# Early loads of chunks 6 and 7, loads behind the transposes in each step, and crossbar transposes for chunks 6 and 7, in a fused retention and feed-forward kernel

One core of one Trainium2 chip. The metric is device time in microseconds (us) of a run; lower is better. A profile gives the span from the first to the last instruction, which is some 1.7 us shorter than the time of the same run (200.26 against 198.6). The granted clock is the share of TensorE's full clock that the trace shows it was given.

## The reference

A recurrent linear attention with a decay per head, then a feed-forward block with a product in place of an activation:

```python
# q, k, v: (4, 8, 768, 64), moe_w1, moe_w2: (512, 1024), w3: (1024, 1024), w_out: (1024, 512)
for t in range(S):
    state = gamma[None, :, None, None] * state + np.einsum('bhd,bhe->bhde', k[:, :, t], v[:, :, t])
    y[:, :, t] = scale * np.einsum('bhd,bhde->bhe', q[:, :, t], state)
x = y.transpose(0, 2, 1, 3).reshape(B * S, H * D)      # 3072 x 512
out = ((x @ w1) * (x @ w2)) @ w3 @ w_out
```

## The kernel before

The kernel folds w3 and w_out into one matrix during the first 31 us, and works through the sequence in 24 chunks of 128 tokens (4 batches of 6). Each chunk needs its queries and keys transposed: chunks 0 to 7 on TensorE, the later ones by transposing DMAs ("by the crossbar"). A step of a chunk computes scores, masks them (VectorE), computes outputs, and pulls matmuls of the feed-forward block in between, so that TensorE has work while other engines answer. All DMAs are issued from one queue (SP; 83408 of the 83430 packets on the page are of its queue q1), in program order: the loads behind the first two stores, at 49.45 and 51.17 us, go out from 51.62 us. Cuts are marked `# ...`.

```python
DT0 = 8                                   # first chunk transposed by the crossbar
for n in range(4, 6):                     # behind the loads of the weights and of chunks 0 to 3
    load_chunk(n)
# ...
def dma_transposes(n):
    if n < DT0 or n >= NSTEP:
        return
    kT = att.tile([128, NP, 128], HP, tag="kT", name="kT", bufs=2)
    nc.sync.dma_start_transpose(kT[:, :, :], k16s[n][:, :])
    # ... even n: the queries of n and n + 1 as well, into qTd

def transposes(n, tag="psT"):
    # ...
    if n >= DT0:
        kT, kp = kTs.pop(n), KP[n % 2]
        nc.scalar.copy(kp[0:64, :, 0, :], kT[0:64, :, :])
        nc.scalar.copy(kp[64:128, :, 1, :], kT[64:128, :, :])
        return
    # ... TensorE transposes into PSUM, then the same two copies

def step(n):
    ready = n * C
    share = fill.available(ready) / (2 - n % 2)
    if n >= DT0 - 2:
        casts(n + 2)                      # GpSimd: q, k, v of chunk n + 2 to 16 bit
    scores(n)
    fill.pull(share * 0.25, ready)
    t_new = kv(n)
    if n < DT0 - 2:
        casts(n + 2)
    dma_transposes(n + 2)
    if n == DT0 - 2:
        load_chunk(n + 4)
    if n % 2:
        q_transposes((n + 1) // 2)        # TensorE, for n + 1 < DT0
    # ...
    outputs(n)
    Tst[0] = t_new
    if n != 4:
        transposes(n + 1)
    fill.pull(share * (0.75 if n == 5 else 0.5), ready)
# ...
load_chunk(6)                             # in program order behind two output stores
load_chunk(7)
# ...
for n in range(4, NSTEP):
    if n != DT0 - 2:
        load_chunk(n + 4)                 # ahead of the step's transposes
    step(n)
```

## Time and profile before

| | before |
|---|---|
| time, first three runs | 198.48, 198.84, 201.69 us (median 198.84) |
| the profiled run | 200.26 us, span 198.6 us, granted clock 0.991 |
| TensorE busy | 187.5 us, 94% |

The slices, windows and timelines that matter are shown in the prediction. In a line of a timeline the columns are start, duration (us), engine, source line, operation, output<-inputs; in brackets is the engine's idle time before it and what ended it.

### The profile page before, as it was taken

The numbers are of one execution on the slowest core, as the hardware profiler recorded it, in microseconds if no ns is written. First come the engines' busy times: TensorE is split into PE (matmuls) and PEld (weight loads), VectorE is DVE, ScalarE is ACT, GpSimd is POOL, SyncE is SP. The second block draws the span as 40 slices with busy tenths as digits, with TensorE's granted clock in tenths as the row PEclk, the third lists the DMA queues.
The fourth block names the chain that finished last, engine by engine and source line by source line (L and its number), as shares of the span: only waits on it lengthen the run. The fifth ranks groups of instructions, "written<-read, shape, count | busy, mean of one in ns | idle before, by whom it ended". The sixth has DMA issues, their size and how long they took to land.

```text
span 198.6 us, 4708 instructions
## 1 busy us (share of the span) xinstructions
PE 187.5 (94%) x1789; PEld 141.9 (71%) x1789; DVE 119.0 (60%) x223; ACT 98.6 (50%) x191; POOL 85.8 (43%) x146
## 2 busy tenths in 40 slices
PE   6899989799999999599999999999999999999993
PEld 2444658486897798388778877787778777887752
DVE  3227596899597666356647665665567665853220
ACT  6478454762445452454455545554546345633322
POOL 7600477827557568244723256646234442200000
PEclk9999999999999999789999999999999999999999
DMA  5999999993699999994998999979999832111014
GB/s 206 377 385 382 311 393 321 373 251 76 178 239 214 195 236 216 210 241 122 199 237 214 190 187 232 201 181 191 204 240 196 175 78 59 56 53 52 35 37 143
DMA packets 83430, 40.15 MB, mean 202 GB/s; under 512 B 59728, under 2 KB 78416, under 8 KB 83408
## 3 DMA queue, kind: packets, MB, share of 16 engines
q1 hardware_dynamic: 83408, 39.86, 86.5%
q8 instruction: 14, 0.23, 0.5%
q14 instruction: 8, 0.07, 0.1%
HBM read 29.36 MB, written 6.29 MB: 180 GB/s over the span
## 4 chain that ended last, share of the span: by engine, by line
PE 66%; DMA 17%; SPq 4%; DVE 3%; POOL 3%; ACT 2%; issue 2%; POOLq 0%; ACTq 0%; DVEq 0%
PE psF L503 32%; PE psO L529 17%; DMA v<-in_v_dram 6%; DMA stg<-in_moe_w_dram 5%; DMA q<-in_q_dram 4%; PE psA L432 4%; SPq L62 4%; DMA kT<-k 3%; PE psY L472 2%; PE psY L473 2%; PE psY L475 2%; PE psK L455 2%; POOL q L327 1%; PE psF L710 1%; PE psW L293 1%
## 5 line engine op out<-in xcount | busy, mean ns | idle before, releaser
L503 PE MATMUL psF<-xt,w 128*128 128x256 f16 (+1 forms) x736 | 86.3, 268 | 0.0
L503 PEld LDWEIGHTS <-w 128*128 128x128 f16 x768 | 68.8, 99 | 7.7
L519 DVE TENSOR_TENSOR ht<-pa,psF 128x256 f16<-128x256 f32 x88 | 36.6, 417 | 27.6 <-PE psF L503 13.8
L513 ACT COPY pa<-psF 128x256 f32<-128x256 f32 x84 | 31.3, 372 | 35.4 <-PE psF L503 35.0
L437 DVE TENSOR_TENSOR am<-psA,keep 128x512 f16<-128x512 f32 x48 | 31.0, 686 | 21.3 <-PE psA L432 21.0
L529 PE MATMUL psO<-w3o,ht 128*128 128x512 f16 x184 | 43.1, 379 | 0.0
L464 POOL TENSOR_TENSOR t<-s,GS 128x512 f16<-128x512 f32 x15 | 19.3, 1285 | 46.6 <-DVE s L463 46.6
L534 ACT ACTIVATE osb<-psO 128x512 f32<-128x512 f32 x23 | 13.8, 598 | 34.4 <-PE psO L529 34.4
L529 PEld LDWEIGHTS <-ht 128*128 128x128 f16 x184 | 17.9, 98 | 17.1 <-DVE ht L759 0.2
L344 POOL TENSOR_TENSOR vp<-v,VS 128x256 f16<-128x256 f32 x40 | 23.8, 616 | 11.7 <-PE psY L475 5.8
L327 POOL CAST q<-q 128x1024 f16<-128x1024 f32 x12 | 13.0, 1087 | 16.2 <-DMA q<-in_q_dram 16.2
L480 DVE TENSOR_TENSOR xt<-psY,YS 128x512 f16<-128x512 f32 x24 | 17.8, 741 | 3.5 <-PE psY L475 3.2
L432 PEld LDWEIGHTS <-kp 128*128 128x128 f16 x192 | 12.7, 99 | 7.5 <-ACT kp L406 2.2
L472 PE MATMUL psY<-am,vp 128*128 128x128 f16 x96 | 16.8, 219 | 0.7 <-ACT kp L230 0.5
L473 PE MATMUL psY<-am,vp 128*128 128x128 f16 x96 | 16.7, 219 | 0.4 <-DVE vp L318 0.4
L340 POOL CAST k<-k 128x512 f16<-128x512 f32 x20 | 12.3, 613 | 7.5 <-PE psK L455 7.0
L463 DVE TENSOR_TENSOR s<-psK,t 128x512 f32<-128x512 f32 x16 | 11.0, 688 | 3.4 <-PE psK L455 3.1
L432 PE MATMUL psA<-qTd,kp 128*128 128x128 f16 x128 | 10.3, 224 | 2.1 <-ACT kp L406 1.7
L406 ACT COPY kp<-kT 64x512 f16<-64x512 f16 x16 | 9.9, 619 | 4.7 <-DMA kT<-k 4.4
L251 DVE COPY w3t<-psW 128x1024 f16<-128x1024 f16 x8 | 5.5, 691 | 10.2 <-PE psW L259 7.9
L473 PEld LDWEIGHTS <-vp 128*128 128x128 f16 x96 | 9.4, 98 | 1.4 <-POOL vp L318 0.7
L475 PE MATMUL psY<-qTd,t 128*128 128x128 f16 x56 | 10.1, 219 | 0.0
(80 smaller groups left out, 198.6 us busy)
## 6 DMA issues: line engine op xcount, KB each, us to landing
stg<-in_moe_w_dram SPq DMA_DIRECT2D x16, 512.0 KB, 7.7
q<-in_q_dram SPq DMA_DIRECT2D x12, 512.0 KB, 4.8
out_dram<-osb SPq DMA_DIRECT2D x23, 256.0 KB, 2.3
k<-in_k_dram SPq DMA_DIRECT2D x20, 256.0 KB, 5.2
v<-in_v_dram SPq DMA_DIRECT2D x20, 256.0 KB, 5.7
stg<-in_moe_w_out_dram SPq DMA_DIRECT2D x4, 512.0 KB, 7.4
stg<-in_k_dram SPq DMA_DIRECT2D x2, 512.0 KB, 10.7
stg<-in_v_dram SPq DMA_DIRECT2D x2, 512.0 KB, 8.2
```

The lines of the kernel that those rows point to most:

```text
L327: nc.gpsimd.tensor_copy(q16[:, :].rearrange("i (t h d) -> i h t d", t=2, d=D), q_in.pop(m)[:, :].rearrange("i (h t d) -> i h t d", t=2, d=D),)
L344: nc.gpsimd.tensor_tensor(vp[:, :, r, r * 64 : r * 64 + 64], v32[:, :].rearrange("j (p s e) -> j p s e", s=2, e=64)[:, :, r, :], VS[:, :]. ...
L432: nc.tensor.matmul(ps[:, i, r, :], lhsT=kp[:, p, r, :], rhs=queries(n, p), start=True, stop=True)
L437: nc.vector.tensor_tensor(am[:, half * 2 : half * 2 + 2, :, :].rearrange("j p s i -> j (p s) i"), ps[:, :, :, :].rearrange("j p s i -> j ( ...
L464: eng.tensor_tensor(t16[:, :, :], s32[:, :, :], GS[:, :, :], MULT)
L472: nc.tensor.matmul(ps[:, p, :], lhsT=vp[:, p, 0, :], rhs=am[:, p, 0, :], start=True, stop=False)
L473: nc.tensor.matmul(ps[:, p, :], lhsT=vp[:, p, 1, :], rhs=am[:, p, 1, :], start=False, stop=(c == 0))
L480: nc.vector.tensor_tensor(XT[n // 2][:, :, n % 2 * C : (n % 2 + 1) * C].rearrange("p a (i t) -> p a t i", t=2), ps[:, :, :].rearrange(orde ...
L503: nc.tensor.matmul(ps[:, i * w : (i + 1) * w], lhsT=W[d][:, (f + i) * 128 : (f + i + 1) * 128], rhs=XT[self.tok0 // TB][:, d, c0 : c0 + w] ...
L513: nc.scalar.copy(self.pa[f][:, :], ps[:, :])
L519: nc.vector.tensor_tensor(self.HT[:, f : f + TB // self.width, :].rearrange("p f n -> p (f n)"), self.pa.pop(f)[:, :], ps[:, :], MULT,)
L529: nc.tensor.matmul(psO[:, :], lhsT=self.HT[:, f, tb * 128 : (tb + 1) * 128], rhs=W3O[f][:, :], start=(f == 0), stop=(f == 7),)
```

## The change

The intent: put the loads of chunks 6 and 7 where the DMA has little to do (a share of 0.15 from 47 to 51.6 us), so that its backlog at chunk 9 goes away; and, as the data is there earlier, let the crossbar take transposes of chunks 6 and 7 from TensorE. Keys of 7 stay on TensorE.

```diff
-    DT0 = 8
+    DT0 = 6
@@
-    for n in range(4, 6):
+    for n in range(4, 8):
         load_chunk(n)
@@
+    def by_dma(n):
+        return n >= DT0 and n != DT0 + 1
@@ dma_transposes, transposes: keys by the crossbar if by_dma(n), not if n >= DT0
@@ step
         dma_transposes(n + 2)
-        if n == DT0 - 2:
-            load_chunk(n + 4)
+        load_chunk(n + 4)
@@
-        if n != 5:
-            fill.pull(share * 0.25, ready)
+        fill.pull(share * 0.25, ready)
@@
-        fill.pull(share * (0.75 if n == 5 else 0.5), ready)
+        fill.pull(share * 0.5, ready)
@@ head: kv(0) moves from ahead of w3_mm(7) into its middle, with scores(1) and outputs(0)
@@
-    load_chunk(6)
-    load_chunk(7)
@@
     for n in range(4, NSTEP):
-        if n != DT0 - 2:
-            load_chunk(n + 4)
         step(n)
```

More of the change, by code (lines that the diff above doesn't have):

```diff
@@ L384, in dma_transposes @@
             return
-        kT = att.tile([128, NP, 128], HP, tag="kT", name="kT", bufs=2)
-        nc.sync.dma_start_transpose(kT[:, :, :], k16s[n][:, :])
-        kTs[n] = kT
+        if by_dma(n):
+            kT = att.tile([128, NP, 128], HP, tag="kT", name="kT", bufs=2)
+            nc.sync.dma_start_transpose(kT[:, :, :], k16s[n][:, :])
+            kTs[n] = kT
         if n % 2 == 0:
@@ L403, in transposes @@
             return
-        if n >= DT0:
+        if by_dma(n):
             kT, kp = kTs.pop(n), KP[n % 2]
@@ L682, with chunk1_scores @@
     scores(0)
-    t_new = kv(0, "psT")
     cast_w(W1, w1_st, 2, False)
-    w3_mm(7, lambda: [scores(1), outputs(0)])
-    Tst[0] = t_new
+    def chunk1_scores():
+        first.append(kv(0, "psT"))
+        scores(1)
+        outputs(0)
+    first = []
+    w3_mm(7, chunk1_scores)
+    Tst[0] = first[0]
     outputs(1, "psT")
```

## The prediction

> **What bounds the kernel now.** I read the page first (busy shares, the slices), then the chain that ended last, then the windows, and only then the timelines of the places where TensorE stops.
>
> ```profile
> PE 187.5 (94%) x1789; PEld 141.9 (71%) x1789; DVE 119.0 (60%) x223; ACT 98.6 (50%) x191; POOL 85.8 (43%) x146
> PE   6899989799999999599999999999999999999993
> PEclk9999999999999999789999999999999999999999
> PE 66%; DMA 17%; SPq 4%; DVE 3%; POOL 3%; ACT 2%; issue 2%; POOLq 0%; ACTq 0%; DVEq 0%
> ```
>
> TensorE is busy 94% of the span, so there is little to win but its idle time and its own work. Of the 11.1 us that it is not busy, the slices show three places: the first 40 us, where weights arrive; one slice at 5 tenths, the 17th (79 to 84 us), which is also where the granted clock dips to 7 and 8 tenths; and the last slice. The windows of four stretches confirm it:
>
> ```profile
> 40.57:79.88 39.31, 39.27 (x466) 32.62 (x465) 29.49 (x55) 16.93 (x35) 24.11 (x33) 1.00 1.03 196
> 79.88:90.57 10.69, 8.54 (x66) 6.32 (x66) 4.65 (x9) 4.83 (x10) 4.13 (x7) 0.84 1.18 221
> 90.57:175.10 84.53, 84.53 (x820) 67.55 (x819) 53.59 (x102) 43.21 (x91) 35.91 (x48) 1.00 0.87 172
> ```
>
> The columns are length, then busy time of TensorE, its weight loads, VectorE, ScalarE and GpSimd, then clock, DMA share and GB/s. From 40.6 to 195 us TensorE never stops except in the middle line. So whatever is saved in that line, and whatever TensorE work goes after 40.6 us, comes off the end one for one. What stops it is in the timelines of TensorE and of ScalarE, and the chain of waits:
>
> ```profile
> 78.16 1.89 PE L529 MATMUL psO<-w3o,ht 128*128 128x512 f16 x8
> 81.80 0.23 PE L432 MATMUL psA<-qTd,kp 128*128 128x128 f16 x1 [1.74 <-ACT kp L406]
> 82.43 0.93 PE L432 MATMUL psA<-qTd,kp 128*128 128x128 f16 x7 [0.41 <-ACT kp L407]
> 83.15 2.77 PE L503 MATMUL psF<-xt,w 128*128 128x256 f16 x12
> 81.12 0.62 ACT L406 COPY kp<-kT 64x512 f16<-64x512 f16 x1 [4.37 <-DMA kT<-k]
> 75.89 5.21 DMA kT<-k
> ```
>
> The scores of chunk 9 wait for the copy of its keys, and the copy for the crossbar transpose that was issued at 75.89 us and took 5.21 us. **The size of the hole:** a step of the steady loop takes 6.56 us from one group of psO matmuls to the next (89.00, 95.56 in the chain); here it took 88.84 - 78.16 = 10.68 us. The loss is 4.12 us: 2.15 us of idle time, the rest the restart at half clock (12 matmuls of 128x256 in 2.56 us of start-to-start time here, 1.31 us in other steps, and scores at the same ratio).
>
> Why was the transpose so late? Its source, the cast of chunk 9's keys, was done at about 68.0 us (the GpSimd timeline has that cast at 67.41, 0.61 long). But the DMA queue's timeline shows an unbroken row of issues from 51.17 to 80.8 us:
>
> ```profile
> 54.24 1.44 SPq L62 DMA_DIRECT2D k<-in_k_dram  x1
> ...
> 56.91 2.46 SPq L62 DMA_DIRECT2D q<-in_q_dram  x1
> ...
> 65.92 1.91 SPq L386 DMA_TRANSPOSE kT<-k  x1
> 67.88 1.29 SPq L390 DMA_TRANSPOSE qTd<-q  x1
> ...
> 74.71 1.09 SPq L536 DMA_DIRECT2D out_dram<-osb  x1
> 75.89 1.23 SPq L386 DMA_TRANSPOSE kT<-k  x1
> ```
>
> The loads of chunks 6 to 9 (51.6 to 64.6), the transposes of 8, the loads of 10 and 11 (69.2 to 74.6) and one store stand in front. The DMA is behind here, and yet it was nearly idle just before: in the window 47 to 51.6 us its share is 0.15, at 57 GB/s. The loads of chunk 6 stood in program order after two output stores that wait for results at 49.4 us.
>
> [...] the first store is issued at 49.45 us, after its copy at 48.82, and no load passes it. [...] Key and value pieces here are 64 floats, 256 B; the page counts 59728 of 83430 packets below 512 B, and the stretch 51.6 to 66 us moves 221 GB/s where the weights moved 370 to 390. [...] a key transpose (128 KB) occupies the queue 1.96 us in the median, a key load of 256 KB 0.70 us. So I count the transposes as dear. [...] here 2.15 us of idle in two pieces were enough to see half rate afterwards, so the dip goes with the idle time and should leave with it.
>
> **The change part by part.**
>
> *Loads of chunks 6 and 7 at once.* 1.5 MB (q 512 KB, two k and two v of 256 KB) move from 51.6 to 56.8 us into the time right after chunk 5's last load, issued at 43.01. They go out from 44 to about 50 us, where the DMA has its hole. At 230 GB/s (estimate from the 221 to 246 of the windows beside) they need 6.5 us and land by 52 to 53 us. Buffers allow it: the third q buffer is free after the cast that ends at 34.2 us.
>
> *Order in a step.* Loads of chunk n+4 are now behind the transposes of n+2 in every step. For chunk 9 that takes the two loads of chunk 11 (2.56 us of issue) out from in front of its transpose.
>
> *New transposes.* Keys of 6 and queries of 6 and 7 add two crossbar transposes to the queue, some 1.9 + 1.3 us by chunk 8's figures, behind the stores at about 54 us. Net for chunk 9: 5.2 us of loads gone from in front, 2.6 us more by the order, 3.2 us added. So its transpose goes out some 4.6 us earlier, at about 71 us, and lands at about 76. The scores need it 1.24 us (two copies of 0.62) ahead of 79.2 us, i.e. at 78. That is 2 us of slack, where it was 3.3 us late. The hole should close whole: **-4.12 us**.
>
> *TensorE work removed.* The instruction order of the changed kernel has 12 matmuls fewer: four transposes of keys 6 (start to start 59.85 to 60.07, 0.22 us) and eight of queries 6 and 7 (58.72 to 59.18, 0.46 us). They lie in the packed stretch: **-0.68 us**. VectorE loses two copies (0.75 us) and ScalarE gains 0.08 us (0.62 for 0.58, twice); neither binds.
>
> *Chunk 1's scores and chunk 0's kv behind four matmuls.* This fills a wait of 0.92 us at 27.5 us. But at 34.25 us the query transposes start just as the cast of those queries ends (34.19), which waited for its load (landed 32.76), and at 35.45 TensorE waits for a key cast. The saved time is waited out there: **0**.
>
> *Pull quota of step 5.* It only reorders matmuls: 0.
>
> Sum: 198.84 - 4.12 - 0.68 = 194.04. I say **194.0 us**, 2.4% less.
>
> **The rivals.**
>
> *The wait moves to chunk 6.* Its transposes are issued only when GpSimd has cast the keys, about 54 us, and the queries' follows at about 56; with the landing times of the page's list (4.5 and 4.1 us, medians in a loaded queue) they arrive at 58.5 and 60. Scores of chunk 6 come at about 61.1. The keys then need 1.24 us on ScalarE. That is 1 us of slack, little. For it: both transposes wait behind two stores and the loads of 6 and 7. [...] If it happens, I expect 0.5 to 1.5 us, and with a clock dip up to 2.5: 195 to 196.5 us.
>
> *The wait moves to chunk 10 or 11.* TensorE comes 4.8 us earlier, while the DMA gets a 5 us head start less 3.2 us for two transposes. In the kernel before chunk 10 had no wait, but its queries landed only at 87.5 us, against a need of 85.8 in the changed one. For the change: its transposes now precede the loads of 12 and the queue should have come to them at 77 to 78 us, landing near 82. The loop later has slack: the queue waits 37.4 us in all for ScalarE's output copies, i.e. for work, not for the DMA. A hole here would cost 1 to 3 us: 195 to 197.
>
> *It was hidden anyway.* If a third thing bounded the end, closing the hole would give nothing. The line 90.57 to 175.10 with 84.53 of 84.53 us busy speaks against it: 199 us, very unlikely.
>
> **Range and chances.** The limit for "faster" is 198.84 x 0.98 = 194.9 us, so a new hole of 0.9 us makes it "same". I give the clean outcome about 0.65, the first rival 0.2, the second 0.13. Some clean-ish outcomes with a few tenths still pass. Range 193.2 (some gain in the head after all) to 196.4 (a new hole with its dip). Faster 0.70, same 0.28, slower 0.02.
>
> **What would show it.** Right: no idle time over 0.3 us on TensorE between 41 and 191 us; clock 1.00 there; DMA share near 1 in 47 to 51.6; chunk 9's key transpose issued near 71 us and landed before 77; 12 matmuls fewer; TensorE's idle time down by some 2 us to about 9. The scores of chunk 6 starting within 0.3 us of the matmul before them clear the first rival; a line of the copy from kT waiting for the DMA names it, or the second, by its time. The prediction is wrong if such a wait appears, with clock below 1.00 behind it, or if the head gets shorter.

## The result, and the profile after

| | before | after |
|---|---|---|
| runs, on the same chip | 198.48, 198.84, 201.61, 201.69 us | 195.81, 195.93, 195.94, 196.04 us |
| median | 200.23 us | 195.94 us |
| fast runs, ratio | 1 | 0.9863 (95%: 0.9839 to 0.9886) |
| profiled run: time, span, clock | 200.26, 198.6 us, 0.991 | 196.04, 194.3 us, 0.998 |

A ratio is the mean time of one kernel's fast runs over that of the other's of the same rounds, so it is not quite the ratio of the medians. A run counts as fast when it is within 1.5% of the fastest of its kernel, which leaves out the two of before above 201 us here. In later sessions most of the long runs of before, at 200 to 201.3 us, stay inside the 1.5%, so ratios of different sessions are not set against each other. The gain that counts is thus 1.4%, where 2.4% was predicted.

The first fence is from the page of the changed kernel (busy tenths and granted clock in 40 slices), the second from its windows (columns as in the prediction).

```profile
PE   6688999879999999999999999999999999999993
PEclk9999999999999999999999999999999999999999
```

```profile
47.00:51.60 4.60, 4.60 (x40) 2.71 (x38) 2.73 (x6) 1.57 (x3) 3.40 (x6) 1.00 0.85 203
79.85:170.00 90.15, 90.15 (x878) 72.33 (x877) 57.78 (x110) 46.49 (x98) 40.98 (x54) 1.00 0.93 186
```

The slice at 5 tenths and the dip of the clock are gone; the DMA's hole at 47 to 51.6 us is filled (203 GB/s where it was 57). Around chunk 9, from the timelines of TensorE, ScalarE and the DMA queue:

```profile
78.12 1.89 PE L534 MATMUL psO<-w3o,ht 128*128 128x512 f16 x8
79.85 0.61 PE L437 MATMUL psA<-qTd,kp 128*128 128x128 f16 x8
73.14 1.21 SPq L391 DMA_TRANSPOSE kT<-k  x1
76.88 0.62 ACT L411 COPY kp<-kT 64x512 f16<-64x512 f16 x1 [0.17 <-DMA kT<-k]
```

The scores of chunk 9 follow the psO matmuls without a pause. The transpose goes out at 73.14 us, not 75.89, and the copy takes it at 76.88; both copies of the keys are done at 78.15, 1.7 us before the scores need them. From 79.85 us on TensorE is busy without a break (90.15 of 90.15 us to 170, and 21.00 of 21.00 us from there to 191). So the mechanism is the predicted one, and by the two profiles alone (198.6 to 194.3 us) even the size seems right. The times say otherwise, and the experiments had to tell why.

### The profile page after: what moved, and what is told of

It reads as the page before. It is cut to its first block, busy times and chain, and to the rows that moved or that the text cites. A ratio compares the mean times of both kernels' runs of the same rounds, so it can differ in the third digit from the quotient of the medians.

```text
span 194.3 us, 4696 instructions
## 1 busy us (share of the span) xinstructions
PE 184.8 (95%) x1777; PEld 139.8 (72%) x1777; DVE 118.3 (61%) x221; ACT 99.1 (51%) x191; POOL 86.4 (44%) x146
## 4 chain that ended last, share of the span: by engine, by line
PE 79%; DMA 10%; DVE 3%; SPq 2%; ACT 2%; POOL 1%; issue 1%; POOLq 0%; ACTq 0%
PE psF L508 39%; PE psO L534 20%; DMA stg<-in_moe_w_dram 5%; PE psA L437 5%; DMA q<-in_q_dram 4%; PE psY L477 3%; PE psY L478 2%; SPq L62 2%; PE psY L480 2%; PE psK L460 2%; DVE am L442 1%; PE psF L719 1%; PE psW L293 1%; PE psG L508 1%; PE psO L551 1%
## 5 line engine op out<-in xcount | busy, mean ns | idle before, releaser
L508 PE MATMUL psF<-xt,w 128*128 128x256 f16 (+1 forms) x736 | 85.0, 266 | 0.0
L411 ACT COPY kp<-kT 64x512 f16<-64x512 f16 x17 | 10.5, 618 | 1.7 <-DMA kT<-k 1.3
L437 PE MATMUL psA<-qTd,kp 128*128 128x128 f16 x144 | 11.1, 219 | 0.0
L480 PE MATMUL psY<-qTd,t 128*128 128x128 f16 x60 | 10.8, 219 | 0.0
```

The source lines that it names most:

```text
L437: nc.tensor.matmul(ps[:, i, r, :], lhsT=kp[:, p, r, :], rhs=queries(n, p), start=True, stop=True)
L480: nc.tensor.matmul(ps[:, p, :], lhsT=Tst[0][:, p, :], rhs=queries(n, p), start=False, stop=True)
L508: nc.tensor.matmul(ps[:, i * w : (i + 1) * w], lhsT=W[d][:, (f + i) * 128 : (f + i + 1) * 128], rhs=XT[self.tok0 // TB][:, d, c0 : c0 + w] ...
```

## The experiments

**Theory A:** the hole before chunk 9's scores has an idle part of about 2.2 us in every run of the kernel before, and in some runs only, TensorE restarts at half clock, for up to 2 us more. The profile I read was of a long run. **Theory B:** the lateness of the transposes itself varies from run to run, the clock does not. **Theory C:** the chip was disturbed in the long runs, whatever the kernel.

### The kernel before, four profiles

No edit: the kernel before.

> The kernel before, unchanged, to see the span and clock of each of its runs (so far 198.48, 198.84, 201.61, 201.69 us). Theory A (the hole at 80 us has a fixed idle part of about 2.2 us, and the half-clock restart of up to 2 us follows in some runs only): times fall in two groups near 198.5 and 201.6, and the group is told by the mean clock (about 0.99 in the longer ones, 1.00 in the shorter). Theory B (the lateness of the transposes itself varies from run to run): times spread, clock alike. Theory C (something outside the hole, a disturbed chip): the changed kernel would have such runs too, which its four runs (195.81 to 196.04) do not show.

> One more profile of the kernel before. Of its 32 timed runs so far 11 took 200 us or more. Two profiles are there: span 198.6 (clock 0.991, hole 4.12 us with half-clock matmuls behind it) and 196.4 (clock 1.00, hole 1.90 us, none at half clock). Theory A: this one falls in line, i.e. a loss of about 2 us with the clock at 1.00, or of more with matmuls at twice their spacing behind the hole and a clock below 1.00; nothing else differs by over 0.7 us. Theory B: a long one with the clock at 1.00.

> As the look before it: another draw, with the same two readings.

The first took 198.14 to 200.44 us in six runs, beside eleven more of 198.36 to 201.48; the two looks took 200.85 and 201.09. The four profiles together ("loss" is the time between the starts of the psO groups around the hole, less the 6.56 us of a step in the steady loop; "idle" is the sum of the two waits of the scores; "first psO" is the start of the first psO group, which shows how late the head was):

| profile | time | span | clock | first psO | idle | loss | loss less idle |
|---|---|---|---|---|---|---|---|
| first | 200.26 | 198.6 | 0.991 | 46.90 | 2.15 | 4.12 | 1.97 |
| before_again | 198.14 | 196.4 | 1.000 | 47.02 | 1.54 | 1.90 | 0.36 |
| before_look1 | 200.85 | 199.1 | 0.991 | 46.92 | 2.58 | 4.59 | 2.01 |
| before_look2 | 201.09 | 199.3 | 0.999 | 48.58 | 2.83 | 3.18 | 0.35 |

TensorE's timeline of before_again, then of before_look1:

```profile
78.27 1.89 PE L529 MATMUL psO<-w3o,ht 128*128 128x512 f16 x8
81.29 0.23 PE L432 MATMUL psA<-qTd,kp 128*128 128x128 f16 x1 [1.13 <-ACT kp L406]
82.33 1.48 PE L503 MATMUL psF<-xt,w 128*128 128x256 f16 x12
86.73 1.89 PE L529 MATMUL psO<-w3o,ht 128*128 128x512 f16 x8
```

```profile
78.18 1.89 PE L529 MATMUL psO<-w3o,ht 128*128 128x512 f16 x8
82.25 0.23 PE L432 MATMUL psA<-qTd,kp 128*128 128x128 f16 x1 [2.17 <-ACT kp L406]
83.49 2.77 PE L503 MATMUL psF<-xt,w 128*128 128x256 f16 x12
89.33 1.89 PE L529 MATMUL psO<-w3o,ht 128*128 128x512 f16 x8
```

The same twelve matmuls behind the hole take 1.48 us in one run and 2.77 us in the other; 2.77 us also in the first profile, where the granted clock from 82.9 to 85.6 us was 0.50. The last column of the table falls in two groups, 0.35 and 2.0 us: the half-clock restart is worth 1.6 us and is there or not. That half of Theory A holds. Its fixed idle part does not: the idle part moves by 1.3 us by itself, as Theory B had it (the transpose went out at 75.69 to 76.39 us in the three profiles with the head on time, and its copy began 4.93 to 5.23 us later). And before_look2 is the longest of the four with the clock whole, the sign named for Theory B; there the head was 1.6 us late (first psO at 48.58), with a load of weights in its chain that took 9.74 us from 32.18 us on, ScalarE waiting 1.84 us for it, and the idle part was the largest. So I expected wrongly that the clock alone tells long from short. It does tell most of them: of the 45 runs of the kernel before whose clock is on record, 14 have 0.991, and these took 199.93 to 201.48 us; of the other 31 only before_look2 took more than 199.46. Over all sessions 16 of 49 timed runs of the kernel before took 200 us or more.

### Keeping TensorE busy through the hole

```diff
 def step(n):
+        if n == DT0 + 1:                  # chunk 9: ahead of its scores
+            psd = ps_t.tile([128, 512], FP, tag="psT", name="psD")
+            for _ in range(10):
+                nc.tensor.matmul(psd[:, :], lhsT=ident16[:, :], rhs=W1[0][:, 0:512], start=True, stop=True)
         scores(n)
```

The result of these matmuls is read by nobody; the kernel's output is correct.

> The kernel before with ten matmuls of 128x512 whose result nobody reads, put ahead of chunk 9's scores: they take 2.16 us, as long as TensorE idles there. Theory A: TensorE does not stop, no half clock follows, and every run is in the short group or below, 198.0 to 199.0 us, none at 201. Theory B: the lateness stays, the dummies change little in the long runs, and some runs are still at 201 or above.

> The kernel before with the dummies in its hole, again: six runs so far, 198.4 to 199.2, none long, where 11 of 32 of the kernel before were at 200 us or more; by chance six without one come up in 8 of 100 cases. Theory A: again none at 200 or above. Theory B: two of six at 200 or above.

198.4 to 199.22 us, and 198.32 to 199.33 the second time (ratios 0.9981 and 0.9976, intervals that include 1). TensorE's timeline in the second:

```profile
80.07 2.32 PE L604 MATMUL psD<-w,ident 128*128 128x512 f16 x10
82.22 0.85 PE L432 MATMUL psA<-qTd,kp 128*128 128x128 f16 x8
87.30 1.89 PE L529 MATMUL psO<-w3o,ht 128*128 128x512 f16 x8
```

The hole is as long as ever (psO from 78.34 to 87.30, a loss of 2.40 us; 2.85 in the first), but it is filled, the clock is 1.00 in both profiles, and no run of twelve reaches 200 us. At the rate of 16 in 49 that would come up by chance about once in 115. Useless work of 2.2 us cost nothing on the median here (198.59 and 198.79 us, beside 198.88 and 198.87 of the kernel before in the same sessions) and took the long runs away: Theory B, under which the dummies change little, falls as the cause of the long runs.

### Early loads alone, new order alone

Both on the kernel before, with TensorE's transposes as they were.

```diff
 loads_only:
-    for n in range(4, 6):
+    for n in range(4, 8):
         load_chunk(n)
-    load_chunk(6)
-    load_chunk(7)
```

```diff
 order_only:
         dma_transposes(n + 2)
-        if n == DT0 - 2:
-            load_chunk(n + 4)
+        load_chunk(n + 4)
@@
-        if n != DT0 - 2:
-            load_chunk(n + 4)
         step(n)
```

> Only the early loads of chunks 6 and 7 in the kernel before; transposes and order as before. Both theories: chunk 9's transpose goes out some 5 us earlier and the hole closes, 195.9 to 196.7 us, with no long runs, if the loads are what matters. If the step order is what matters, the hole stays, 198 us or more.

> Only the order within a step (loads of chunk n+4 behind the transposes of n+2) in the kernel before. By the queue's issue times chunk 9's transpose moves 2.6 us earlier, to 73.3, and lands at 78.5, where 78.0 would do: a hole of 0.5 us is left, 196.5 to 197.5 us. If the DMA's backlog and not the place in the queue decides, it lands as late as before: 198.5 us.

196.27 us median (196.01 to 197.09; ratio 0.9869) and 196.29 (196.13 to 196.48; ratio 0.9858), in the same session. Each closes the hole alone; together they cannot do it twice. I had expected order_only to leave half a microsecond. The DMA queue and the copy of chunk 9's keys in order_only:

```profile
73.10 1.24 SPq L386 DMA_TRANSPOSE kT<-k  x1
76.91 0.62 ACT L406 COPY kp<-kT 64x512 f16<-64x512 f16 x1
```

The issue came where I put it (73.3 expected), but the copy starts at 76.91 without waiting: the transpose landed within 3.8 us of its issue, where in the kernel before it took 5.21. Taking two loads (2.56 us of issue) from in front of this one transpose is enough; why it also landed sooner after its issue is not separated. In loads_only I had expected the transpose some 5 us earlier; it went out at 73.85, 2.04 us earlier, and that of chunk 8 at 63.62, 2.30 us earlier; what took the rest of the 5 us is not shown. Its copy began at 77.61 us, still in time.

### The crossbar part alone

The changed kernel with DT0 = 8 and the exception for chunk 7 removed, so that TensorE transposes chunks 6 and 7; loads, order and head as changed.

```diff
-    DT0 = 6
+    DT0 = 8
-        return n >= DT0 and n != DT0 + 1
+        return n >= DT0
```

> The changed kernel with chunks 6 and 7 transposed by TensorE again (early loads, new order and new head kept). It measures the crossbar part alone. The prediction's working: 0.68 us slower than the changed kernel, 196.6 us. What the changed kernel's trace suggests instead: the eight query transposes had filled a wait for VectorE's mask in step 5, so only the four key transposes (0.22 us) and some 0.1 us count: 196.2 to 196.3 us.

196.31 us median (ratio 0.9859). Times of different sessions (on different chips, in part) do not separate a third of a microsecond, but the traces do, since the stretch from the first psO group to the scores of chunk 8 leaves the head out. Its ends, before and in the changed kernel:

```profile
46.90 3.62 PE L529 MATMUL psO<-w3o,ht 128*128 128x512 f16 x16
73.33 0.61 PE L432 MATMUL psA<-qTd,kp 128*128 128x128 f16 x8
```

```profile
47.20 3.62 PE L534 MATMUL psO<-w3o,ht 128*128 128x512 f16 x16
73.29 0.61 PE L437 MATMUL psA<-qTd,kp 128*128 128x128 f16 x8
```

The stretch is 26.43 us before, 26.42 in loads_order (46.98 to 73.40), 26.09 in the changed kernel (again 26.09 in a second profile, 47.05 to 73.14). **The crossbar saves 0.33 us, not 0.68.** Step 5 in TensorE's timeline, before and after:

```profile
58.07 0.61 PE L503 MATMUL psF<-xt,w 128*128 128x128 f16 x8
58.72 0.62 PE L366 MATMUL psTq<-ident,q 128*128 128x128 f16 x8
59.18 0.22 PE L472 MATMUL psY<-am,vp 128*128 128x128 f16 x1
```

```profile
58.38 0.61 PE L508 MATMUL psF<-xt,w 128*128 128x128 f16 x8
59.10 0.22 PE L477 MATMUL psY<-am,vp 128*128 128x128 f16 x1
59.38 0.22 PE L480 MATMUL psY<-qT,t 128*128 128x128 f16 x1
59.70 0.22 PE L477 MATMUL psY<-am,vp 128*128 128x128 f16 x1
```

Before, the eight query transposes stood between the feed-forward matmuls and the outputs, and ran while VectorE masked the scores (from 58.05 to 59.34 us). With them gone the outputs start 0.72 us behind the start of the feed-forward matmuls (1.11 before), and then halt once more, between 59.38 and 59.70, for the second half of the mask (VectorE works on it from 58.35 to 59.64).

### The loads late again

```diff
 on the changed kernel:
-    for n in range(4, 8):
+    for n in range(4, 6):
         load_chunk(n)
@@
+    load_chunk(6)
+    load_chunk(7)
     fill.run(2)
     casts(5)
```

> The changed kernel with the loads of chunks 6 and 7 put back where they were (behind the first two stores), crossbar for 6 and 7 kept. If the early loads are what lets the crossbar take over chunk 6: its keys are cast only at about 58.6 us (as before), the transposes go out behind the loads and land at 63 to 65, and TensorE, which wants chunk 6 at 61.3, stops for 2.5 to 4 us there: 198.5 to 200.5 us. If not, it is as the changed kernel, 196.

199.77 us median (199.29 to 201.43; ratio 1.0042): the median is in the expected range, but TensorE stops elsewhere. Its timeline, and GpSimd's:

```profile
63.28 0.29 PE L480 MATMUL psY<-qT,t 128*128 128x128 f16 x1 [3.00 <-POOL t L469]
57.19 1.04 POOL L327 CAST q<-q 128x1024 f16<-128x1024 f32 x1 [3.72 <-DMA q<-in_q_dram]
58.47 0.61 POOL L340 CAST k<-k 128x512 f16<-128x512 f32 x1 [0.25 <-DMA k<-in_k_dram]
60.82 1.19 POOL L344 TENSOR_TENSOR vp<-v,VS 128x256 f16<-128x256 f32 x2 [1.74 <-DMA v<-in_v_dram]
61.97 1.26 POOL L469 TENSOR_TENSOR t<-s,GS 128x512 f16<-128x512 f32 x1
```

To feed the crossbar in time, the casts of chunk 6 stand ahead of the state of chunk 4 in GpSimd's order. When their loads are late, GpSimd waits, the state (t) comes late, and TensorE stops for 3.00 us in chunk 5's outputs, a step ahead of the place that I had named, and runs at about half rate behind it: the next matmuls of the outputs start 0.106 us apart, where the step before had 0.05 to 0.06, the eight psO matmuls take 2.99 us, where the other profiles have 1.89, and the mean clock of the run is 0.991. So the early loads are needed once the crossbar takes chunk 6; without them the change is worth nothing.

### The head as it was

```diff
 on the changed kernel:
+    t_new = kv(0, "psT")
     cast_w(W1, w1_st, 2, False)
@@ the helper chunk1_scores goes
-    w3_mm(7, chunk1_scores)
-    Tst[0] = first[0]
+    w3_mm(7, lambda: [scores(1), outputs(0)])
+    Tst[0] = t_new
```

> The changed kernel with the head as it was (chunk 0's kv ahead of the last w3 product). The prediction's working: no difference (195.9), since TensorE waits for a load at 34 us anyway. A rival: the 0.9 us wait is worth something at the end, up to 0.9 us slower, 196.8.

196.37 us median (195.7 to 196.98), beside 195.94 and 196.22 of the changed kernel in other sessions; a few tenths either way are not excluded by time. The wait of kv(0) is back (1.36 us in this profile), the first psO group starts at 47.07 (47.20 and 47.05 in the two profiles of the changed kernel): the traces show no gain from this part, as predicted.

### Variants that go further

```diff
 refill, on the changed kernel:
-        fill.pull(share * 0.5, ready)
+        fill.pull(share * (0.25 if n == 4 else 0.5), ready)
 refill_keys: that, and
-        return n >= DT0 and n != DT0 + 1
+        return n >= DT0
```

> The changed kernel with one quota changed: at the end of step 4 half as many feed-forward matmuls are pulled, so that eight of 128x128 stand between chunk 5's scores and outputs, where the changed kernel's trace shows TensorE waiting 0.33 us for the mask. If that wait is what swallowed half of the 0.68 us, the time falls by 0.2 to 0.33 us, to 195.6 to 195.75; if VectorE bounds the step, no change.

> The changed kernel with the quota of the refill run and with the keys of chunk 7 by the crossbar too: 0.22 us of TensorE work less. If its transpose lands in time (issue near 61, landing near 65, needed at 65.5) the stretch from the first psO matmul to the scores of chunk 8 gets 0.2 us shorter than in the refill run (25.92 us there) and the time 0.2 us, hardly to be told from the noise. If it lands late, TensorE stops at the scores of chunk 7 for 0.5 us or more.

refill: 196.2 us median (195.59 to 197.07). The stretch from the first psO group to the scores of chunk 8 is 25.92 us (47.77 to 73.69), 0.17 less than in the changed kernel, so the wait for the mask is partly filled; in time it does not show. refill_keys: 195.83 us (195.67 to 196.16), ratio 0.9828; its stretch is 25.66 us (46.99 to 72.65).

> The variant with the changed quota and the keys of 7 by the crossbar, beside the changed kernel in the same rounds. The traces say 0.43 us less from the first psO matmul to the scores of chunk 8 (25.66 against 26.09). In time: 0.2 to 0.6 us below the changed kernel's median of these rounds.

> The changed kernel, unchanged. If the long runs of the kernel before come from its hole (idle part and half-clock restart), there are none over 197.2 us here: what is left is the head, whose lateness varied by 1.7 us over the profiles. If they come from the chip, one third of the runs is 2 us or more above the rest.

Side by side: refill_keys 196.04 us (195.68 to 197.21), the changed kernel 196.22 (195.83 to 197.91), and the kernel before 198.18 to 198.85 in its four runs. 0.18 us is less than the spread and than the 0.2 expected, so a better kernel is not shown by time. In this second profile of refill_keys the stretch is 25.91 us (47.48 to 73.39), not 25.66, and the keys of chunk 7 came too late once:

```profile
66.87 0.56 PE L437 MATMUL psA<-qTd,kp 128*128 128x128 f16 x7 [0.17 <-ACT kp L412]
```

which shows how little slack there is. One run of the changed kernel, 197.91, broke my expectation of none over 197.2. Of the 52 timed runs of kernels without the hole (the changed one, loads_only, order_only, loads_order, old_head, and the two refills) it is the longest; they span 195.59 to 197.91, where the 49 runs of the kernel before span 198.08 to 201.69. What was late in that one run is not known, as it was not profiled; Theory C, though, would have put a third of these runs 2 us or more above the rest, and falls.

## Why the prediction was wrong

- **What bounds the kernel: right.** What was saved ahead of chunk 9's scores came off the end; TensorE is busy 90.15 of 90.15 us behind chunk 9's scores.
- **"The size of the hole", and the -4.12 us: the step that failed.** The number is read correctly from the profile, and was then taken off 198.84, the median of other runs. The profiled run took 200.26 us. From each profiled run's own time the working comes out (time, less its loss, less 0.33 for the crossbar): 200.26 - 4.12 - 0.33 = 195.81, 198.14 - 1.90 - 0.33 = 195.91, 200.85 - 4.59 - 0.33 = 195.93, and 201.09 - 3.18 - 0.33 = 197.58, of which the late head is 1.6. The changed kernel took 195.94. For the two fast runs, the term is about 2.4 as a remainder, not as a reading: 198.66 (their mean) less 195.93 (the mean of the changed kernel's) is 2.73, less 0.33. Neither of them was profiled. Two signs were there beforehand: a time of the profiled run that was 1.4 us off the median, and three runs that spread by 3.2 us.
- **"The dip goes with the idle time": right when there is a dip.** It was taken as part of every run; it is in two of four profiles, and worth 1.6 us there.
- **Loads and order as the cure: right, but counted as a sum.** Either one alone closes the hole. The transpose was predicted to go out at about 71 us and went at 73.14; it still landed ahead of its use. The loads of chunks 6 and 7 had gone out from 45.06 to 53.19 us, not from 44 to 50. (A slip without effect: by the prediction's own figures the landing had been 81.1 - 78 = 3.1 us late, not 3.3.)
- **Transposes counted as dear: not shown.** The 1.96 and 0.70 us are times for which an issue held the queue, waits included; they are not speeds of transfer. In the changed kernel the key transposes hold it for 1.22 us in the median. From issue to landing the medians of the kernel before are 4.5 us for a key transpose (128 KB) and 5.2 us for a key load (256 KB).
- **"TensorE work removed", -0.68 us: half of it.** All 12 matmuls are gone, but the eight query transposes had been running in a wait for the mask, so -0.33 us remained. The prediction treated the stretch as packed because it showed almost no idle time; the work that filled the wait was the very work removed.
- **The head, 0: fits** (old_head: no gain in the traces).
- **First rival, the wait moves to chunk 6: did not happen,** but was near: ScalarE waited 1.14 us for the keys of chunk 6, and had copied them by 60.91, with the scores at 61.76. With late loads a stop of 3.00 us did appear, through GpSimd.
- **Second rival, a wait at chunk 10 or 11: did not happen.** The line of 90.15 busy us rules it out. (The queries of chunk 10 had landed 3.9 us after their issue at 83.33, so at 87.2 us, not 87.5.)

What stays open is what decides, run by run, whether the half clock follows: idle times of 2.15, 2.58 and (in late_loads) 3.00 us had it, 1.54 and 2.83 had not. What sets the lateness of the head in a run is open too.

## What to carry to other kernels

Set a stall that you read from a profile against the time of that same run, not against the median of others; where runs of the kernel spread by more than the stall's worth, profile it more than once before you size the gain. Work that filled a wait cost nothing here (2.2 us of it in fill_hole, without a loss on the median), and removing 0.68 us of transposes, of which 0.46 had filled one, gained 0.33: look for what stands behind the removed instructions, and what it waits for, even where the engine shows no idle time. In this queue, issued in program order, the place of one urgent transfer mattered as much as what stood in front of it: a ratio of 0.9858 in order_only, of 0.9869 in loads_only.
